# Four heads' last keys in one attention unit, and token groups of 768, 512 and 512 with 512-column products

## The chip, the cores and the metric

The program runs on one core of a Trainium2 chip. The metric is the device time of one execution in microseconds (us). PE is TensorE, which multiplies; PEld is its row of weight loads, shown beside PE; DVE is VectorE, ACT is ScalarE, and SP is the engine whose queue issues every DMA here.

## What is computed

Attention with a sigmoid in place of the softmax (4 batches, 12 heads, 448 tokens, 64 values a head), and behind it two feed-forward layers over all 4 x 448 = 1792 tokens. All arrays are fp32; the layers' weights arrive as 64-bit numbers.

```python
scores = scale * np.matmul(q, k.transpose(0, 1, 3, 2)) - np.log(S)
attn = 1.0 / (1.0 + np.exp(-scores))
x = np.matmul(attn, v)               # then to (1792 tokens, 768)
...
h = x @ w_in                         # 768 -> 2048
g = s * np.maximum(h, 0.0) ** 2 + b
x = g @ w_out                        # 2048 -> 768
...
h = x @ w_in2
g = np.maximum(h, 0.0) + alpha * np.minimum(h, 0.0)
out = g @ w_out2
```

## The kernel before

**Attention.** Two heads make a pair; there are 24 pairs, and each has its K and Q (one tile, 64 rows a head) and its V in a buffer of four. A pair's 448 keys are cut into chunks `c` = 0 to 3 of 128, 128, 128 and 64 keys, and one chunk of one pair is a unit `u`. In a unit the array is used as four quadrants of 64 x 64: `emit_qk` (L234) gives one fp32 product to each quadrant (two heads `j`, two halves `h` of the chunk), `emit_sig` (L248) takes the sigmoid of the scores on ACT, and `emit_av` (L257) gives again four products, two units later. A unit with `c` = 3 has only 64 keys, so it has `h` = 0 alone: two products of scores and two of values. One fp32 product shows as two records in the profile, since it goes over the array twice. `emit_x` (L274) adds the two halves of a finished pair on ACT and DVE. Sixteen units `conv_step` (L307) also turn a weight block from 64 to 32 bits on DVE (`convert`, L123). The loads of pair `q+3` are written in the third unit of pair `q` (L319), so ten units before the first product that reads them.

**Layers.** The tokens go in two groups (`PASSES`, L20) of 896, two batches of 448 each, through each layer `m`. In a pass the 16 blocks of `w_in` are 16 steps and the 6 x 3 cuts of `w_out` are 18 steps (`PER` = 34). Every fp32 operand is split into two numbers of a narrower format (fp32r) whose sum it is, `hi` and `lo`; a chunk of 128 x 128 weights then takes three products for each batch, hi x hi, hi x lo and lo x hi, all into one accumulator: that is `three` (L339), six products of 448 columns. Each product loads its weights anew.

**What feeds the steps.** `split_unit` (L170) makes `hi` on ACT and `lo` on DVE from a 32-bit weight block, two steps ahead; `fetch` (L433) starts the load of a block two steps before that, or converts it where it is used for the first time (`JUST`). `ahead` (L454) converts the first blocks of the second layer in steps 36 to 66. `in_evac` (L360) takes a step's sums out of PSUM, applies the layer's function and splits the result `g`; the `s` and `b` of the first layer are put on after the second product, with a sum that two more columns of `g` (of ones) give (L377, L403). Two PSUM pools of two tiles take turns, so four accumulators are in hand. The order on every engine is the order in which the code is written.

Of the kernel before, what the change touches and what calls it, by code (L numbers as in the profile page):

```python
# [16 lines left out]
P = 128  # L17
OUT_CUTS = [(0, 6), (6, 11), (11, 16)]

PASSES = [(0, 0), (0, 1), (1, 0), (1, 1)]  # L20
# [13 lines left out]
def tile_kernel(  # L34
# [23 lines left out]
    T2 = 2 * S  # L58
    NCUT = len(OUT_CUTS)
    PER = NFC + NK * NCUT  # L60
    LAST = S - (NCH - 1) * P
# [9 lines left out]
    wrawp = pool("wraw", 3)  # L71
    whlp = pool("whl", 3)
    tp = pool("tp", 3)
# [10 lines left out]
    def t_tile(name):  # L84
        return tp.tile([P, T2], F32, tag="t", name=name)

    def g_tile(fc, name="g"):
        return gp.tile([P, 2 * T2 + 2], F32, tag=f"g{fc}", name=f"{name}{fc}")

# [10 lines left out]
    bsum = const.tile([P, NK], F32, name="bsum")  # L100
# [90 lines left out]

    def x_tile(kc):
        x[kc] = xp.tile([P, 2, 2, S], F32R, tag=f"x{kc}", name=f"x{kc}")
        return x[kc]

    def x_store(key, shape_cols, name):
        if key not in x_dram:
            x_dram[key] = dram.tile([P, 2, S], F32, tag=name, name=name)
        return x_dram[key]


    NU = B * NPR * NCH
# [14 lines left out]
    def where(u):  # L217
        q, c = divmod(u, NCH)
        bb, pr = divmod(q, NPR)
        return q, bb, pr, c  # L220
# [13 lines left out]
    def emit_qk(u):  # L234
        q, bb, pr, c = where(u)
        t = kqt[q]
        sc = acc_tile("sc")
        for h in range(2 if c < NCH - 1 else 1):
            for j in range(2):
                rows = slice(j * D, (j + 1) * D)  # L240
                keys = slice(c * P + h * D, c * P + (h + 1) * D)
                nc.tensor.matmul(  # L242
                    sc[h * D : (h + 1) * D, j, :S], t[rows, keys], t[rows, S:],
                    start=True, stop=True,
                )
        sct[u] = sc

    def emit_sig(u):  # L248
        c = u % NCH
        n = P if c < NCH - 1 else LAST  # L250
        sg = buffer("sg", T2).rearrange("p (j s) -> p j s", j=2)
        nc.scalar.activation(  # L252
            sg[:n], sct.pop(u)[:n, :, :S], AF.Sigmoid, bias=bias_t[:n, 0:1], scale=QKSCALE
        )
        sgt[u] = sg

    def emit_av(u):  # L257
        q, bb, pr, c = where(u)
        if c == 0:
            avt[q] = av_tile("av")  # L260
        sg = sgt.pop(u)

        for h in range(2 if c < NCH - 1 else 1):
            for j in range(2):
                keys = slice(h * D, (h + 1) * D)
                nc.tensor.matmul(  # L266
                    avt[q][j * D : (j + 1) * D, h, :S],
                    vtt[q][keys, j, c, :],
                    sg[keys, j, :],
                    start=(c == 0),  # L270
                    stop=(c == NCH - 1 - h),
                )

    def emit_x(q):  # L274
# [5 lines left out]
        if bb < 2:  # L280
            if bb == 0:
                x_tile(pr)
            split(x[pr][:, 1, bb], x[pr][:, 0, bb], t, "V")
        else:
            stores.append((x_store((0, 1, pr), S, f"xa{pr}")[:, bb - 2], t))
# [10 lines left out]
    nc.scalar.activation(bsum[:, 0:1], bias_t, AF.Sigmoid)  # L296
# [10 lines left out]
    conv_step = {4 + (k * 88) // NFC: k for k in range(NFC)}  # L307
    for u in range(NU + 2):
# [8 lines left out]
        if u % NCH == 1 and u > NCH:  # L317
            emit_x(u // NCH - 1)
        if u % NCH == 2:  # L319
            load_kq(u // NCH + 3)  # L320
            load_v(u // NCH + 3)
# [27 lines left out]
    def in_mm(fc, i):  # L349
        hp[fc] = (acc_tile, av_tile)[fc % 2]("hps")  # L350
        w = whl.pop(i)
        for kc in range(NK):
            cols = slice(kc * P, (kc + 1) * P)
            three(
                hp[fc], (S, S), (w[:, 0, cols], w[:, 1, cols]),
                [[x[kc][:, e, bk] for bk in range(2)] for e in range(2)],
                kc == 0, kc == NK - 1,
            )

    def in_evac(m, p, fc):  # L360
        h = hp.pop(fc)[:, :, :S]
        t = t_tile("t")
        t3 = t.rearrange("p (b s) -> p b s", b=2)
        if m == 0:
            nc.scalar.activation(t3, h, AF.Relu)  # L365
            nc.scalar.activation(t, t, AF.Square)  # L366
        else:
            n = t_tile("n")
            nc.scalar.activation(t3, h, AF.Relu)  # L369
            nc.scalar.activation(n.rearrange("p (b s) -> p b s", b=2), h, AF.Relu, scale=-1.0)  # L370
            nc.vector.scalar_tensor_tensor(  # L371
                out=t, in0=n, scalar=nal_t[:, fc : fc + 1], in1=t, op0=ALU.mult, op1=ALU.add
            )
        gt = g_tile(fc)
        if (m, p) == PASSES[0]:

            nc.vector.memset(gt[:, 2 * T2 :], 1.0)  # L377
        gt = gt.bitcast(F32R)
        split(gt[:, T2 : 2 * T2], gt[:, :T2], t, "VA"[m])
        g[fc] = gt  # L380

    def out_mm(dc, cut, i, sums):
        c0, c1 = OUT_CUTS[cut]
        if c0 == 0:
            op_[dc] = (acc_tile, av_tile)[dc % 2]("ops")
        w = whl.pop(i)
        for fc in range(c0, c1):
            o = (fc - c0) * P
            gt = g[fc]
            three(  # L390
                op_[dc], (S, S + 2 if sums else S), (w[:, 0, o : o + P], w[:, 1, o : o + P]),
                [[gt[:, :S], gt[:, S:T2]], [gt[:, T2 : 3 * S], gt[:, 3 * S :]]],
                fc == 0, fc == NFC - 1,
            )

    def out_evac(m, p, dc):
        o = op_.pop(dc)
        t = t_tile("o")
        t3 = t.rearrange("p (b s) -> p b s", b=2)
        if m == 0:  # L400

            if p == 0:
                nc.scalar.activation(  # L403
                    bsum[:, dc : dc + 1], o[:, 1, S : S + 1], AF.Copy, scale=b_t[:, 0:1]
                )
            nc.scalar.activation(
                t3, o[:, :, :S], AF.Identity, scale=s_t[:, 0:1], bias=bsum[:, dc : dc + 1]
            )
            dst = x_store((1, p, dc), T2, f"x2_{p}_{dc}").rearrange("p b s -> p (b s)")
        else:  # L410
            nc.scalar.copy(t3, o[:, :, :S])  # L411
            dst = out[dc * P : (dc + 1) * P, p * T2 : (p + 1) * T2]
        stores.append((dst, t))

    def load_xr(key):
        xr[key] = t_tile("xr")
        nc.sync.dma_start(out=xr[key], in_=x_dram[key].rearrange("p b s -> p (b s)"))

    def make_x(key):
        t = x_tile(key[2])  # L420
        split(
            t[:, 1].rearrange("p b s -> p (b s)"), t[:, 0].rearrange("p b s -> p (b s)"),
            xr.pop(key), "A",
        )
# [29 lines left out]
    ahead = {PER + 2 + 2 * k: PER + k for k in range(NFC)}  # L454

    n_split, n_fetch = 2, 4
    pend = None
    for n, st in enumerate(steps):
# [4 lines left out]
        if kind == "in":  # L463
            in_mm(c, n)
        else:
            out_mm(c, cut, n, o == 0)
# [64 lines left out]
```

## Time and profile before

| | |
|---|---|
| runs of the kernel | 1100.80, 1102.32, 1100.18 us; median 1100.8 |
| the profiled execution's own time | 1100.52 us |
| span of its profile | 1098.7 us |
| attention, from the first product to the first product of the layers | 4.20 to 151.05 us |
| eight phases of the layers (in and out, four passes) | 116.93, 117.11, 119.04, 117.37, 119.03, 117.37, 119.03 and 117.38 us |
| from the last product to the span's end | 4.4 us |
| busy share of the span | PE 99%, PEld 85%, DVE 41%, ACT 39% |

The span is read from left to right as attention, then for each layer and pass a phase `hps` (16 steps, w_in) and a phase `ops` (18 steps, w_out). A matmul's end in the profile is modelled, so its record is longer than the time to the next one; the spacing of starts, or a phase's time over its count, tells what one product costs. The granted clock of TensorE is 1.00, that is 2.4 GHz, in every window asked for.

### The profile page before, as it was taken

How to read it: one execution, taken by the hardware profiler on the slowest of the kernel's cores; microseconds unless marked ns; L12 is line 12 of the kernel's file. 1: busy time of each engine (PE TensorE's matmuls, PEld its weight loads, DVE VectorE, ACT ScalarE, POOL GpSimd, SP SyncE). 2: the span in 40 equal slices, each digit the busy share in tenths (PEclk: the TensorE clock that was granted, in tenths of full speed). 3: DMA queues.
4: the chain of work that ended last, by engine and by line, in shares of the span. 5: the costliest groups of instructions: out<-in, count | busy, mean ns of one | idle time of the engine just before them, and what ended most of it. 6: DMA issues, size and time to landing. Idle time of an engine off the chain costs nothing.

```text
span 1098.7 us, 14184 instructions
## 1 busy us (share of the span) xinstructions
PE 1090.1 (99%) x5952; PEld 930.7 (85%) x5952; DVE 449.6 (41%) x567; ACT 433.9 (39%) x519; POOL 0.2 (0%) x4
## 2 busy tenths in 40 slices
PE   8999999999999999999999999999999999999998
PEld 3444469999999999999999999999999999999997
DVE  3664433346455144544333244375552234431110
ACT  6777753334333134342323244453331344431110
POOL 0000000000000000000000000000000000000000
PEclk9999999999999999999999999999999999999999
DMA  6878720004677433344565511146773111122210
GB/s 248 303 266 309 241 111 1 1 11 145 216 212 223 146 99 120 117 137 141 185 211 187 180 53 48 44 118 184 242 220 116 60 58 58 41 65 67 84 55 34
DMA packets 46864, 147.22 MB, mean 134 GB/s; under 512 B 5584, under 2 KB 7120, under 8 KB 46800
## 3 DMA queue, kind: packets, MB, share of 16 engines
q1 hardware_dynamic: 46800, 146.31, 40.9%
q8 instruction: 47, 0.77, 0.3%
q14 instruction: 17, 0.14, 0.0%
HBM read 107.36 MB, written 38.93 MB: 133 GB/s over the span
## 4 chain that ended last, share of the span: by engine, by line
PE 99%; DMA 0%; ACT 0%; issue 0%
PE hps L344 43%; PE ops L344 43%; PE sc L242 7%; PE av L266 7%; DMA ga<-in_kq 0%; ACT o L411 0%
## 5 line engine op out<-in xcount | busy, mean ns | idle before, releaser
L344 PE MATMUL hps<-x,whl 128*128 128x448 f32 x2304 | 474.6, 367 | 0.0
L344 PE MATMUL ops<-g,whl 128*128 128x448 f32 (+1 forms) x2304 | 469.9, 365 | 0.0
L344 PEld LDWEIGHTS hps<-x,whl 128*128 128x128 f32 x2304 | 432.5, 188 | 42.0 <-issue 0.7
L344 PEld LDWEIGHTS ops<-g,whl 128*128 128x128 f32 x2304 | 432.6, 188 | 36.6
L95 DVE TENSOR_TENSOR whl<-wraw,whl 128x768 fp32r<-128x768 f32 (+1 forms) x120 | 108.3, 902 | 272.4 <-ACT whl L92 272.4
L92 ACT CAST whl<-wraw 128x768 fp32r<-128x768 f32 (+1 forms) x120 | 94.5, 787 | 204.3 <-PE ops L344 186.7
L242 PE MATMUL sc<-ga 64*64 64x448 f32 x672 | 143.9, 555 | 4.2 <-DMA ga<-in_kq 4.2
L266 PE MATMUL av<-ga,ga 64*64 64x448 f32 x672 | 142.2, 540 | 0.0
L252 ACT ACTIVATE ga<-sc,bias_t 128x896 f32<-128x896 f32 x96 | 96.6, 1007 | 40.8 <-PE sc L242 28.9
L365 ACT ACTIVATE t<-hps 128x896 f32<-128x896 f32 x32 | 29.4, 918 | 145.1 <-PE hps L344 145.1
L95 DVE TENSOR_TENSOR g<-t,g 128x896 fp32r<-128x896 f32 x64 | 69.9, 1093 | 33.4 <-ACT g L92 32.3
L242 PEld LDWEIGHTS sc<-ga 64*64 64x64 f32 x672 | 44.6, 134 | 44.5 <-issue 34.8
L371 DVE SCALAR_TENSOR_TENSOR t<-n,nal_t,t 128x896 f32<-128x896 f32 x32 | 36.9, 1152 | 104.1 <-ACT n L370 104.1
L266 PEld LDWEIGHTS av<-ga,ga 64*64 64x64 f32 x672 | 44.9, 133 | 40.1 <-issue 39.3
L94 DVE CAST g<-t 128x896 fp32r<-128x896 f32 x32 | 20.1, 627 | 130.8 <-ACT t L366 130.8
L369 ACT ACTIVATE t<-hps 128x896 f32<-128x896 f32 x32 | 29.4, 918 | 93.1 <-PE hps L344 93.1
L140 DVE SCALAR_TENSOR_TENSOR cva<-r,cva 128x768 f32<-128x768 f32 (+1 forms) x68 | 61.7, 907 | 0.6
L92 ACT CAST g<-t 128x896 fp32r<-128x896 f32 x32 | 30.1, 942 | 39.0 <-DVE t L371 39.0
L134 ACT ACTIVATE cva<-r 128x768 f32<-128x768 f32 (+1 forms) x52 | 44.4, 853 | 0.0
L411 ACT COPY o<-ops 128x896 f32<-128x896 f32 x12 | 10.9, 907 | 70.8 <-PE ops L344 57.1
L279 DVE TENSOR_TENSOR xo<-av,xo 128x448 f32<-128x448 f32 x24 | 15.0, 625 | 57.4 <-ACT xo L278 57.3
L148 DVE SCALAR_TENSOR_TENSOR wraw<-cva,wraw 128x640 uint32<-128x640 uint32 (+1 forms) x36 | 31.3, 870 | 1.2
(26 smaller groups left out, 242.9 us busy)
## 6 DMA issues: line engine op xcount, KB each, us to landing
r<-in_w_in SPq DMA_DIRECT2D x32, 768.0 KB, 5.4
wraw<-w SPq DMA_DIRECT2D x60, 384.0 KB, 3.0
r<-in_w_out SPq DMA_DIRECT2D x24, 640.0 KB, 4.8
ga<-in_kq SPq DMA_DIRECT2D x24, 448.0 KB, 6.6
r<-in_w_out SPq DMA_DIRECT2D x12, 768.0 KB, 5.5
w<-wraw SPq DMA_DIRECT2D x24, 320.0 KB, 5.7
wraw<-w SPq DMA_DIRECT2D x24, 320.0 KB, 3.0
ga<-in_vt SPq DMA_DIRECT2D x24, 256.0 KB, 6.8
```

Source lines behind the costliest of these rows:

```text
L92: nc.scalar.copy(hi, src)
L95: nc.vector.tensor_tensor(out=lo, in0=src, in1=hi.bitcast(F32), op=ALU.subtract)
L134: nc.scalar.activation(a.bitcast(F32), hi.bitcast(F32), AF.Relu, scale=-(2.0**-80))
L140: nc.vector.scalar_tensor_tensor(out=a.bitcast(F32), in0=hi.bitcast(F32), scalar=2.0**-112, in1=a.bitcast(F32), op0=ALU.mult, op1=ALU.max,)
L148: nc.vector.scalar_tensor_tensor(out=u, in0=a, scalar=3, in1=u, op0=ALU.logical_shift_left, op1=ALU.bitwise_or,)
L242: nc.tensor.matmul(sc[h * D : (h + 1) * D, j, :S], t[rows, keys], t[rows, S:], start=True, stop=True,)
L252: nc.scalar.activation(sg[:n], sct.pop(u)[:n, :, :S], AF.Sigmoid, bias=bias_t[:n, 0:1], scale=QKSCALE)
L266: nc.tensor.matmul(avt[q][j * D : (j + 1) * D, h, :S], vtt[q][keys, j, c, :], sg[keys, j, :], start=(c == 0), stop=(c == NCH - 1 - h),)
L344: nc.tensor.matmul(dst[:, bk, :c], w[a], mv[m][bk][:, :c], start=first and k == 0, stop=last and k == 2,)
L365: nc.scalar.activation(t3, h, AF.Relu)
L369: nc.scalar.activation(t3, h, AF.Relu)
L371: nc.vector.scalar_tensor_tensor(out=t, in0=n, scalar=nal_t[:, fc : fc + 1], in1=t, op0=ALU.mult, op1=ALU.add)
```

## The change

- A unit with `c` = 3 now takes the last 64 keys of two pairs, the even pair `q` on one half of the quadrants and pair `q+1` on the other: seven units for two pairs, not eight, 84 in all. The loads of pair `q+3` stay in the third unit of pair `q`, which is now eight units ahead of their first product.
- The tokens go in three groups of 768, 512 and 512 (`TOK`). A chunk of a 512-token group takes three products of 512 columns. A chunk of the 768-token group takes five: the last 256 columns of `hi` and of `lo` lie side by side and go as one product of 512 into two halves of a PSUM bank, which `take` adds up afterwards on DVE; only lo x hi of the last 256 columns goes alone.
- Each weight block is loaded and split six times instead of four. `s` and `b` are applied on DVE in `in_evac`, and the two columns of ones go.
- The pools of raw weights, split weights and temporary tiles have four buffers instead of three, raw blocks are fetched one step earlier, and `ahead` converts every fourth step instead of every second.

```diff
-PASSES = [(0, 0), (0, 1), (1, 0), (1, 1)]
+PASSES = [(0, 0), (0, 1), (0, 2), (1, 0), (1, 1), (1, 2)]
+N5 = 512
...
+    REST = B * S - 3 * N5
+    TG = N5 + REST
+    TOK = [TG, N5, N5]
...
-    wrawp = pool("wraw", 3)
-    whlp = pool("whl", 3)
-    tp = pool("tp", 3)
+    wrawp = pool("wraw", 4)
+    whlp = pool("whl", 4)
+    tp = pool("tp", 4)
...
+    def parts(t):
+        return t[:, N5 : N5 + TG], [(t[:, :N5], 0, N5), (t[:, N5 + TG :], N5, TG)]
...
-    NU = B * NPR * NCH
+    order = []
+    for q in range(0, B * NPR, 2):
+        order += [(q, c) for c in range(NCH)] + [(q + 1, c) for c in range(NCH - 1)]
+    NU = len(order)
...
+    def tiles(u):
+        q, c = order[u]
+        if c == NCH - 1:
+            return [(h, q + h, c * P) for h in range(2)]
+        return [(h, q, c * P + h * D) for h in range(2)]
...
-        for h in range(2 if c < NCH - 1 else 1):
+        for h, q, k0 in tiles(u):
...
-        if u % NCH == 2:
-            load_kq(u // NCH + 3)
-            load_v(u // NCH + 3)
+        if u < NU and order[u][1] == 2:
+            load_kq(order[u][0] + 3)
+            load_v(order[u][0] + 3)
...
-    def three(dst, n, w, mv, first, last):
-        for k, (a, m) in enumerate(((0, 1), (0, 0), (1, 1))):
-            for bk in range(2):
-                c = n[bk] if m == 1 else S
-                nc.tensor.matmul(
-                    dst[:, bk, :c], w[a], mv[m][bk][:, :c],
-                    start=first and k == 0, stop=last and k == 2,
-                )
+    def three(dst, p, w, mv, first, last):
+        hi, lo = w
+        nc.tensor.matmul(dst[:, :N5], hi, mv[:, N5 : 2 * N5], start=first, stop=False)
+        nc.tensor.matmul(dst[:, :N5], hi, mv[:, :N5], start=False, stop=False)
+        if p == 0:
+            nc.tensor.matmul(dst[:, N5 : 2 * N5], hi, mv[:, 2 * N5 :], start=first, stop=False)
+        nc.tensor.matmul(dst[:, :N5], lo, mv[:, N5 : 2 * N5], start=False, stop=last)
+        if p == 0:
+            nc.tensor.matmul(dst[:, N5:TG], lo, mv[:, 2 * N5 : N5 + TG], start=False, stop=last)
...
+    def take(h, p, name):
+        t = t_tile(name)[:, : TOK[p]]
+        nc.scalar.copy(t, h[:, : TOK[p]])
+        if p == 0:
+            nc.vector.tensor_tensor(out=t[:, N5:], in0=h[:, TG:], in1=t[:, N5:], op=ALU.add)
+        return t
...
+            if p == 0:
+                t = take(h, p, "t")
+                nc.vector.scalar_tensor_tensor(
+                    out=t, in0=t, scalar=0.0, in1=t, op0=ALU.max, op1=ALU.mult
+                )
+            else:
+                t = t_tile("t")[:, :N5]
+                nc.scalar.activation(t, h[:, :N5], AF.Relu)
+                nc.scalar.activation(t, t, AF.Square)
+            nc.vector.tensor_scalar(
+                out=t, in0=t, scalar1=s_t[:, 0:1], scalar2=b_t[:, 0:1], op0=ALU.mult, op1=ALU.add
...
-        split(gt[:, T2 : 2 * T2], gt[:, :T2], t, "VA"[m])
+        split_to(g[fc], t, 0, "A" if p == 0 else "V")
...
-    ahead = {PER + 2 + 2 * k: PER + k for k in range(NFC)}
-    n_split, n_fetch = 2, 4
+    ahead = {PER + 2 + 4 * k: PER + k for k in range(NFC)}
+    n_split, n_fetch = 2, 5
```

PE in the attention, second and third pair, before (`sc` scores, `av` values; ga_93 to ga_96 hold K and Q of four pairs, ga_97 to ga_101 sigmoids, ga_102 to ga_105 V):

```order
L266 MATMUL av<-ga_98,ga_102 64x448 x4
L242 MATMUL sc<-ga_94 64x448 x4
L266 MATMUL av<-ga_99,ga_102 64x448 x4
L242 MATMUL sc<-ga_94 64x448 x4
L266 MATMUL av<-ga_100,ga_102 64x448 x2
L242 MATMUL sc<-ga_94 64x448 x4
L266 MATMUL av<-ga_101,ga_103 64x448 x4
L242 MATMUL sc<-ga_94 64x448 x2
L266 MATMUL av<-ga_97,ga_103 64x448 x4
L242 MATMUL sc<-ga_95 64x448 x4
```

The same place of the changed kernel:

```order
L276 MATMUL sc<-ga_93 64x448 x2
L276 MATMUL sc<-ga_94 64x448 x2
L302 MATMUL av<-ga_98,ga_102 64x448 x4
L276 MATMUL sc<-ga_94 64x448 x4
L302 MATMUL av<-ga_99,ga_102 64x448 x4
L276 MATMUL sc<-ga_94 64x448 x4
L302 MATMUL av<-ga_100,ga_102 64x448 x2
L302 MATMUL av<-ga_100,ga_103 64x448 x2
L276 MATMUL sc<-ga_94 64x448 x4
L302 MATMUL av<-ga_101,ga_103 64x448 x4
L276 MATMUL sc<-ga_95 64x448 x4
```

The two products that stood alone (x2) now stand beside two of the next pair, whose buffer is thus first read one unit before its own first chunk.

PE at the beginning of the first layer, before (`hps` the accumulator, x_ the tokens of one chunk of 128 inputs; the last row of the attention stands ahead):

```order
L266 MATMUL av<-ga_97,ga_105 64x448 x2
L344 MATMUL hps<-x_189,whl 128x448 x6
L344 MATMUL hps<-x_234,whl 128x448 x6
L344 MATMUL hps<-x_288,whl 128x448 x6
L344 MATMUL hps<-x_342,whl 128x448 x6
```

The same place of the changed kernel, in its group of 768 tokens:

```order
L302 MATMUL av<-ga_100,ga_105 64x448 x4
L382 MATMUL hps<-x_194,whl 128x512
L383 MATMUL hps<-x_194,whl 128x512
L385 MATMUL hps<-x_194,whl 128x512
L386 MATMUL hps<-x_194,whl 128x512
L388 MATMUL hps<-x_194,whl 128x256
L382 MATMUL hps<-x_232,whl 128x512
```

Six products of 448 became four of 512 and one of 256 here; in the groups of 512 tokens the rows L382, L383 and L386 alone repeat.

DVE in the second pass of the first layer, two steps of which one converts a block ahead, before (`g` the split results, `whl` the split weights, `cw` the converted block):

```order
L94 CAST g_3257<-t 128x896
L95 TENSOR_TENSOR g_3257<-t,g_3257 128x896
L95 TENSOR_TENSOR whl<-wraw,whl 128x768
L94 CAST g_3305<-t 128x896
L95 TENSOR_TENSOR g_3305<-t,g_3305 128x896
L95 TENSOR_TENSOR whl<-wraw,whl 128x768
L140 SCALAR_TENSOR_TENSOR cva<-r_3107,cva 128x768
L145 TENSOR_SCALAR cw<-r_3107 128x768
L148 SCALAR_TENSOR_TENSOR cw<-cva,cw 128x768
```

Two such steps of the changed kernel, in its first group of 512 tokens:

```order
L417 TENSOR_SCALAR t<-t,s_t,b_t 128x512
L210 CAST g_3151<-t 128x512
L215 TENSOR_TENSOR g_3151<-t,g_3151 128x512
L101 TENSOR_TENSOR whl<-wraw,whl 128x768
L146 SCALAR_TENSOR_TENSOR cva<-r_2897,cva 128x768
L151 TENSOR_SCALAR cw<-r_2897 128x768
L154 SCALAR_TENSOR_TENSOR cw<-cva,cw 128x768
L417 TENSOR_SCALAR t<-t,s_t,b_t 128x512
L210 CAST g_3192<-t 128x512
L215 TENSOR_TENSOR g_3192<-t,g_3192 128x512
L101 TENSOR_TENSOR whl<-wraw,whl 128x768
```

A step handles 512 columns of results and not 896, with one operation more, while its weight split is as large as it was; the conversion stands in one step of four.

## Rows read from the trace of the kernel before

**Rows 1.** The page: engines' busy time (share) x instructions; the chain's shares.

```profile
PE 1090.1 (99%) x5952; PEld 930.7 (85%) x5952; DVE 449.6 (41%) x567; ACT 433.9 (39%) x519; POOL 0.2 (0%) x4
PE 99%; DMA 0%; ACT 0%; issue 0%
```

**Rows 2.** The chain in order of time: start, length (us), what.

```profile
0.73 3.42 DMA ga<-in_kq
4.20 4.76 PE sc L242 x24
...
18.00 0.38 PE av L266 x3
...
72.12 0.38 PE av L266 x3
...
151.05 116.93 PE hps L344 x576
267.98 117.11 PE ops L344 x576
385.09 119.04 PE hps L344 x576
504.13 117.37 PE ops L344 x576
...
976.93 117.38 PE ops L344 x576
1094.34 0.91 ACT o L411
```

**Rows 3.** Waits: engine, line waited for: us in total, times, longest; all of PE's.

```profile
PE sc L242 <- DMA ga<-in_kq: 4.2, 1, 4.2
```

**Rows 4.** The page's groups, weight loads: xcount | busy us, mean ns | idle before.

```profile
L344 PEld LDWEIGHTS hps<-x,whl 128*128 128x128 f32 x2304 | 432.5, 188 | 42.0 <-issue 0.7
L344 PEld LDWEIGHTS ops<-g,whl 128*128 128x128 f32 x2304 | 432.6, 188 | 36.6
L242 PEld LDWEIGHTS sc<-ga 64*64 64x64 f32 x672 | 44.6, 134 | 44.5 <-issue 34.8
```

**Rows 5.** Windows: stretch, length, PE, PEld, DVE, ACT, POOL busy, clock, DMA share, GB/s.

```profile
4.00:151.00 147.00, 146.80 (x1345) 65.66 (x1345) 73.76 (x113) 107.61 (x121) 0.00 (x0) 1.00 0.77 270
385.00:504.00 119.00, 119.00 (x578) 108.07 (x577) 55.73 (x67) 46.60 (x55) 0.00 (x0) 1.00 0.38 125
```

**Rows 6.** Windows within the attention, same columns.

```profile
96.00:108.00 12.00, 12.00 (x116) 5.36 (x112) 4.97 (x7) 8.90 (x10) 0.00 (x0) 1.00 1.03 402
```

**Rows 7.** SP's issues from 20 us (pairs 5 and 6): start, us, what.

```profile
24.79 0.33 SPq L120 DMA_DIRECT2D r<-in_w_in  x1
25.78 0.33 SPq L158 DMA_DIRECT2D w<-ga  x1
26.20 0.38 SPq L226 DMA_DIRECT2D ga<-in_kq  x1
...
27.69 0.76 SPq L226 DMA_DIRECT2D ga<-in_kq  x1
```

**Rows 8.** PE's timeline at pair 5's first product, and landing times of attention's loads.

```profile
34.44 0.55 PE L242 MATMUL sc<-ga 64*64 64x448 f32 x3
...
DMA to landing us min/median/max: 2.9/6.6/9.1
```

**Rows 9.** Groups by form, ACT and DVE: xcount | busy us, mean ns | idle before.

```profile
L252 ACT ACTIVATE ga<-sc,bias_t 128x896 f32<-128x896 f32 x72 | 72.6, 1008 | 29.7 <-PE sc L242 17.8 <-PE av L266 10.0 <-ACT xo L278 0.4
L95 DVE TENSOR_TENSOR whl<-wraw,whl 128x768 fp32r<-128x768 f32 x72 | 68.7, 954 | 118.0 <-ACT whl L92 118.0
L92 ACT CAST whl<-wraw 128x768 fp32r<-128x768 f32 x72 | 59.7, 829 | 120.2 <-PE ops L344 109.9 <-issue 10.3
L140 DVE SCALAR_TENSOR_TENSOR cva<-r,cva 128x768 f32<-128x768 f32 x44 | 42.0, 956 | 0.6
L134 ACT ACTIVATE cva<-r 128x768 f32<-128x768 f32 x28 | 25.4, 907 | 0.0
L278 ACT COPY xo<-av 128x448 f32<-128x448 f32 x24 | 12.6, 523 | 0.5 <-PE av L266 0.5
L95 DVE TENSOR_TENSOR x<-xo,x 128x448 fp32r<-128x448 f32 x12 | 7.5, 625 | 0.4
L94 DVE CAST x<-xo 128x448 fp32r<-128x448 f32 x12 | 4.7, 394 | 0.4
L145 DVE TENSOR_SCALAR cw<-r 128x768 uint32<-128x768 uint32 x16 | 8.9, 554 | 0.0
L148 DVE SCALAR_TENSOR_TENSOR cw<-cva,cw 128x768 uint32<-128x768 uint32 x16 | 15.3, 959 | 0.6
```

More of the change, by code (lines that the diff above doesn't have):

```diff
@@ L234, in emit_qk @@
     def emit_qk(u):
[L235 to L236 removed]
         sc = acc_tile("sc")
[L238 removed]
+        for h, q, k0 in tiles(u):
             for j in range(2):
                 rows = slice(j * D, (j + 1) * D)
[L241 removed]
                 nc.tensor.matmul(
[L243 removed]
+                    sc[h * D : (h + 1) * D, j, :S],
+                    kqt[q][rows, k0 : k0 + D],
+                    kqt[q][rows, S:],
                     start=True, stop=True,
@@ L257, in emit_av @@
     def emit_av(u):
-        q, bb, pr, c = where(u)
-        if c == 0:
-            avt[q] = av_tile("av")
+        c = order[u][1]
         sg = sgt.pop(u)
-        for h in range(2 if c < NCH - 1 else 1):
+        for h, q, _ in tiles(u):
+            if q not in avt:
+                avt[q] = av_tile("av")
+            first = c == (NCH - 1 if q % 2 and h else 0)
+            last = c == (NCH - 1 if not q % 2 and not h else NCH - 2)
             for j in range(2):
@@ L269, in emit_av @@
                     sg[keys, j, :],
-                    start=(c == 0),
-                    stop=(c == NCH - 1 - h),
+                    start=first, stop=last,
                 )
@@ L279, in emit_x @@
         nc.vector.tensor_tensor(out=t, in0=av[:, 1, :S], in1=t, op=ALU.add)
[L280 to L285, printed above, removed]
+        if bb == 0:
+            x_tile(pr)
+        for p in range(3):
+            a, e = max(bb * S, TOK0[p]), min((bb + 1) * S, TOK0[p] + TOK[p])
+            if a < e:
+                src = t[:, a - bb * S : e - bb * S]
+                if p == 0:
+                    split_to(x[pr], src, a, "V")
+                else:
+                    stores.append((x_store(0, p, pr)[:, a - TOK0[p] : e - TOK0[p]], src))
     def flush_stores():
@@ L306, in tile_kernel @@
     next64()
-    conv_step = {4 + (k * 88) // NFC: k for k in range(NFC)}
+    conv_step = {4 + (k * (NU - 8)) // NFC: k for k in range(NFC)}
     for u in range(NU + 2):
@@ L316, in tile_kernel @@
         store32()
-        if u % NCH == 1 and u > NCH:
-            emit_x(u // NCH - 1)
-        if u % NCH == 2:
-            load_kq(u // NCH + 3)
-            load_v(u // NCH + 3)
+        if u >= 2:
+            q, c = order[u - 2]
+            if c == NCH - 1 - q % 2:
+                emit_x(q)
+        if u < NU and order[u][1] == 2:
+            load_kq(order[u][0] + 3)
+            load_v(order[u][0] + 3)
         if u in conv_step:
@@ L396, in out_evac @@
     def out_evac(m, p, dc):
-        o = op_.pop(dc)
-        t = t_tile("o")
-        t3 = t.rearrange("p (b s) -> p b s", b=2)
+        t = take(op_.pop(dc), p, "o")
         if m == 0:
[L402 to L409, printed above, removed]
-        else:
-            nc.scalar.copy(t3, o[:, :, :S])
-            dst = out[dc * P : (dc + 1) * P, p * T2 : (p + 1) * T2]
+            dst = x_store(1, p, dc)
+        else:
+            dst = out[dc * P : (dc + 1) * P, TOK0[p] : TOK0[p] + TOK[p]]
@@ L413, in out_evac @@
         stores.append((dst, t))
     def load_xr(key):
-        xr[key] = t_tile("xr")
-        nc.sync.dma_start(out=xr[key], in_=x_dram[key].rearrange("p b s -> p (b s)"))
+        xr[key] = t_tile("xr")[:, : TOK[key[1]]]
+        nc.sync.dma_start(out=xr[key], in_=x_dram[key])
     def make_x(key):
[L420 to L424, printed above, removed]
+        split_to(x_tile(key[2]), xr.pop(key), 0, "A")
```

108 lines of the change are left out of this document (58 added, 50 removed).

## The prediction

> **What bounds the kernel now.** First the engines' busy time: PE is busy 99% of the span, DVE 41%, ACT 39% [rows 1]. Then the chain of waits: all but its ends is PE, and PE waits once in the whole program, 4.2 us for the first K and Q [rows 2, 3]. So only what shortens PE's own row counts, and the question is what one product costs. There are two kinds.
>
> In the attention the chain shows the same point of the rhythm at 18.00 and at 72.12 us [rows 2], nine pairs of heads later: 54.12 / 9 = 6.013 us a pair. A pair has four units, each a round trip of scores and values; in rounds of the four quadrants that is 4 x 4 = 16, of 375.8 ns. A product goes over the array twice, and 2 x 448 columns at 2.4 GHz (the granted clock is 1.00 [rows 5]) are 373.3 ns. Here a product costs its columns and 2.5 ns, and the unit with two quadrants idle costs as much as a full one: with cheaper short units the pair would need 14 rounds, 5.26 us.
>
> In the layers a phase takes 576 products: 116.93 to 119.04 us [rows 2], so 203.0 to 206.7 ns each, 204.7 in the mean of the eight. But 448 columns at 2.4 GHz are 186.7 ns. What fills the other 18? The weight loads: 188 ns each, and the row of loads is idle only 42.0 and 36.6 us over 2304 of them [rows 4], that is 18 and 16 ns. Load and gap together, 432.5 + 42.0 = 474.5 us, are the whole time of the four `hps` phases. I read a chain: a load begins when the product before it has begun, takes 188 ns, and its own product follows 16 to 18 ns behind. In the attention a load of half the columns takes 134 ns [rows 4] under a product of 376, so nothing waits for it. **The layers are thus bound by the weight loads at 448 columns**, just above what the columns need, and a product of 512 (213.3 ns, and 2.5 as in the attention: 215.8) would be bound by its columns, with the load below it.
>
> **Attention, step by step.** 96 units become 84. Twelve units of 4 rounds at 375.8 ns go: 12 x 1.503 = 18.0 us. ACT has to follow: in two pairs seven sigmoids of 1.008 and two copies of 0.523 [rows 9] are 8.1 us under 7 x 1.503 = 10.5 us of PE; it is 77% busy, as before.
> What could come late is a load. It is written eight units ahead of its use, not ten: 12.0 us, not 15.0. In SP's queue it stands behind the reload of a 64-bit block, which waits for the conversion on DVE, and behind the block's store. Where conversion and the end of a pair meet in the unit before, that costs most: the load of pair 5 (counted from 0) is issued at 26.20 and first used at 34.44 [rows 7, 8], 8.2 us later. Take 3.0 from it and 5.2 us remain, against a landing of 6.6 us in the median and 9.1 at most [rows 8]. In the new order units 8 and 61 have that coincidence, each one unit ahead of a load. Each costs between nothing (a landing below 5.2; the shortest is 2.9) and 3.9 us; the median gives 1.4. There is also the denser traffic: the stage moved at a share of 0.77 [rows 5], and the same bytes in 131 us make 0.86; full share does occur, 402 GB/s [rows 6]. I take 2 us for the stage, bounds 0 and 8.
> Attention: 146.85 - 18.0 + 2 = 130.8 us.
>
> **The layers' products.** A chunk of weights had 12 products in its two groups, now 5 + 3 + 3. There are 384 chunks (96 in each of `in` and `out`, in two layers), so 4608 products become 3840 of 512 columns and 384 of 256. The columns are the same in sum, 2,064,384. By the reading above the 512s cost 215.8 ns; the 256s are far below the load and cost what the load chain does, 204.7. No row shows a product of 256 at this size; its bounds are its columns and the gap behind the load, 106.7 + 18 = 125, and 206.7, the dearest phase; I take 204.7, since a load of the same size stands behind it. (125 would save 31 us more, but it needs two loads in 341 ns, and the rows show none of them faster than 188.)
> 3840 x 215.8 = 828.7, and 384 x 204.7 = 78.6: 907.3 us, for 943.3 measured (the eight phases). **Saved: 36.0 us.** By phases: 96 x (4 x 215.8 + 204.7) = 102.5 us for 768 tokens, 96 x 3 x 215.8 = 62.2 for 512. Bounds of the 512: 213.3, the bare columns, and 218, if some of the jitter of 203 to 207 is left: -10 and +8 us.
>
> **What must keep up.** Weight blocks are loaded and split 204 times, not 136. A step of six chunks of 512 tokens is 18 x 215.8 ns = 3.88 us. DVE in it, by the nearest rows scaled to 512 columns [rows 9]: weight split 0.95, the new `s`, `b` operation 0.37 (554 at 768), cast 0.45 (394 at 448), difference 0.71 (625 at 448): 2.5 us, and every fourth step a conversion of 0.956 + 0.554 + 0.959 = 2.5, so 3.1 in the mean. ACT: split 0.83 and two operations of 0.60 (523 at 448), 2.0. Both fit; a step with a conversion takes DVE 5.0, but splits are two steps ahead. A fetch of 384 KB per 3.88 us is 101 GB/s, far below the 402 that was moved.
> In the 768-token group the step is 6.41 us. DVE: addition 0.4, two operations of 0.96 and 0.55, differences 1.1, split 0.95 and a wait for ACT's cast of 0.8, 4.8 in all; in the five steps 11 to 15 of each layer, which convert too, 7.2, so DVE falls 4 us behind under a lead of two steps, 12.8. I take 0.5 us for all of it, bounds 0 and 6. The two columns of ones and the bias chain go from ACT and DVE, which hid them: nothing. The last copy is 512 columns, not 896, 0.60 for 0.91, and its store is smaller: the tail is 4.0 for 4.4.
>
> **The sum** against the profiled execution, whose span is 1098.7 and whose own time 1100.52, 0.3 below the median of the runs: 4.2 + 130.8 + 907.3 + 0.5 + 4.0 = 1046.8, and 1.8 around the span: 1048.6. I say **1049 us**, 52 less.
>
> **The rivals.**
> *A fixed price on every product.* If the 18 ns are not the load but come on top of the columns, whatever they are, the 512s cost 231.4 and the 256s 124.8: 888.6 + 47.9 = 936.5 us, 29.2 more than forecast: 1078. For it: the gap is there in every phase. Against: the attention's products show 2.5 ns.
> *Columns alone.* If fp32r streams more slowly than one column a cycle, 204.7 for 448, equal columns cost equal time, the layers stay at 943.3, and only the attention gains: 1085. Against it speaks the attention's rhythm, which keeps the clock. A page would have it likewise: the Trainium skill, TensorE: Matmul & The Clock Gate, gives a gap of columns / 2.4 + 2.5 ns (section "Back-to-back issue gap") and a load of columns / 1.2, 107 ns here (section "LDWEIGHTS (loading the stationary operand)"), so no load would bind, and 384 products fewer would save 1 us, an estimate from that page. The trace does not agree on either: 188 ns a load, and 203 to 207 ns where its gap gives 189.
> *The loads hold the attention.* If pairs come in as late as the traffic lets them and the shorter lead fails at every pair, the stage stays near its old length, and up to 16 of the 18 us are lost: 1057 to 1065. It decides where lag and landing exceed 12.0 us in most pairs; for pair 5 they make 34.44 - 26.20 too short, for the rest the only wait in rows 3 speaks against it.
> *The feed falls behind: slower.* Place: the 64 `in` steps of the 512-token groups. If ACT and DVE wait for each other in every step, their times add up: 2.0 + 2.5 and a quarter of a conversion (2.5, and 0.9 on ACT) in the first layer, 5.4 us; 4.9 in the second, where an operation of 0.71 stands for the 0.37 and nothing is converted. The mean, 5.1, is 1.2 above the step: +77 us, 1126. From 3.88 us a step it costs, and from 4.73 (54 us over 64 steps on top) the change is slower than before. Against it: in a window with the same code DVE is busy 55.7 and ACT 46.6 of 119 us [rows 5] and PE does not wait.
>
> **How the numbers follow.** Forecast 0.76; fixed price 0.09; columns alone 0.04; attention held 0.07; feed 0.04. The forecast's own range: down 10 for the columns' lower bound, of which I take half since the attention shows 2.5 ns, and 2 for no late load: 1042; up 8 by the attention and 8 by the jitter, not both whole: 1058. With the attention held it reaches 1066. What is left out is the fixed price, columns alone, the feed and a little below, 0.2. So 1042 to 1066. A measurement tells 0.2%, 2.2 us, from no change. Faster than that: all cases but the feed, 0.96. Of the feed's 0.04 I give 0.01 to a loss that just eats the gain, and 0.03 to slower.
>
> **What would show it.** The phases: 102.5 and 62.2 us, without waits on PE. Loads still at 188 ns, but with 28 ns between them under a product of 512, and the product after a 256 starting about 205 ns later. If the fixed price is right, the phases are 100.8 and 66.6. The attention ends at 135 us, with one or two short waits for a K and Q load, near units 9 to 17 and 62 to 70; if it ends at 150 the loads hold it. Waits of PE for `whl` in the 512-token groups would show the feed. The forecast falls if a 512 costs over 218 ns or the attention loses over 8 us to loads.

## The result, and the profile after

The changed kernel took 1061.1 us in the median of four runs (1060.42 to 1061.98), the one before 1100.5 beside it: a ratio of 0.964, 95% interval 0.9623 to 0.9657. That is 39.4 us less; forecast were 52, in a range that holds the time near its upper end. The profiled execution took 1060.63 us with a span of 1058.8. Its parts, by the trace:

| part of the span | before | forecast | after |
|---|---|---|---|
| to the first product | 4.2 | 4.2 | 4.1 |
| attention | 146.8 | 130.8 | 128.6 |
| layers, with the feed | 943.3 | 907.8 | 922.6 |
| tail | 4.4 | 4.0 | 3.7 |

So the attention came out 2.2 us better than forecast and the layers 14.8 us worse. The page, in the order of [rows 1]:

```profile
PE 1051.1 (99%) x5568; PEld 814.4 (77%) x5568; DVE 594.4 (56%) x879; ACT 448.9 (42%) x625; POOL 0.2 (0%) x4
```

PE is as full as it was; DVE has 145 us more to do, and PE waits for none of it. All that PE waits for is still one load, as in [rows 3]:

```profile
PE sc L276 <- DMA ga<-in_kq: 4.0, 1, 4.0
```

The windows (columns as in [rows 5]) of the attention, of a phase with 768 tokens and of two with 512:

```profile
4.00:132.60 128.60, 128.55 (x1344) 48.64 (x1344) 72.64 (x119) 95.71 (x109) 0.00 (x0) 1.00 0.88 311
132.70:232.70 100.00, 100.00 (x484) 83.36 (x481) 67.67 (x102) 38.12 (x50) 0.00 (x0) 1.00 0.13 38
332.80:398.00 65.20, 65.20 (x289) 53.99 (x289) 47.42 (x74) 34.04 (x51) 0.00 (x0) 1.00 0.46 150
398.10:463.30 65.20, 65.20 (x289) 53.99 (x288) 30.67 (x40) 23.25 (x35) 0.00 (x0) 1.00 0.71 239
```

A phase of 768 tokens takes 100.0 us (forecast 102.5), one of 512 takes 65.3 (forecast 62.2), and each kind is alike within 0.13. The two phases of 512 tokens take the same time although DVE is busy 47.4 us of one and 30.7 of the other and the DMA share is 0.46 and 0.71, so the price of a product does not follow what the other engines or the transfers do. The products are neither what I said of the 512s nor of the 256s. PE's and PEld's timeline, start and length, around one product of 256 (L388) in a 768-token phase:

```profile
200.09 0.39 PE L386 MATMUL hps<-x,whl 128*128 128x512 f32 x1
200.10 0.19 PEld L388 LDWEIGHTS hps<-x,whl 128*128 128x128 f32 x1
...
200.32 0.28 PE L388 MATMUL hps<-x,whl 128*128 128x256 f32 x1
200.32 0.19 PEld L382 LDWEIGHTS hps<-x,whl 128*128 128x128 f32 x1
200.44 0.40 PE L382 MATMUL hps<-x,whl 128*128 128x512 f32 x1
200.44 0.19 PEld L383 LDWEIGHTS hps<-x,whl 128*128 128x128 f32 x1
```

The load for L382 begins at 200.32 and is drawn to 200.51, but its product begins at 200.44. A product does not wait for the end of its load's record. With that the chain that I read out of [rows 4] is gone: the 256 costs 117 ns, not 204.7. And in a 512-token phase, where the load (188 ns) has 25 ns to spare, the products still do not come at 215.8:

```profile
350.21 0.39 PE L386 MATMUL hps<-x,whl 128*128 128x512 f32 x1
350.44 0.39 PE L382 MATMUL hps<-x,whl 128*128 128x512 f32 x1
350.67 0.39 PE L383 MATMUL hps<-x,whl 128*128 128x512 f32 x1
350.89 0.39 PE L386 MATMUL hps<-x,whl 128*128 128x512 f32 x1
```

Three spacings in 0.68 us; over a phase, 65.28 us / 288 = 226.7 ns, 13.3 over the columns (512 at 2.4 GHz, 213.3). The runs below ask what these 13.3 ns are, whether the two parts of the change add up, and whether the feed and the loads were as near the edge as I had priced them.

### The profile page after: what moved, and what is told of

Its sections match the earlier page's. It is cut to its first block, busy times and chain, and to the rows that moved or that the text cites. A ratio compares the mean times of both kernels' runs of the same rounds, so it can differ in the third digit from the quotient of the medians.

```text
span 1058.8 us, 14149 instructions
## 1 busy us (share of the span) xinstructions
PE 1051.1 (99%) x5568; PEld 814.4 (77%) x5568; DVE 594.4 (56%) x879; ACT 448.9 (42%) x625; POOL 0.2 (0%) x4
## 4 chain that ended last, share of the span: by engine, by line
PE 99%; DMA 0%; ACT 0%; issue 0%
PE hps L383 12%; PE ops L383 12%; PE hps L382 12%; PE ops L382 12%; PE ops L386 12%; PE hps L386 12%; PE sc L276 6%; PE av L302 6%; PE ops L385 4%; PE hps L385 4%; PE ops L388 2%; PE hps L388 2%; DMA ga<-in_kq 0%; ACT o L400 0%
## 5 line engine op out<-in xcount | busy, mean ns | idle before, releaser
L101 DVE TENSOR_TENSOR whl<-wraw,whl 128x768 fp32r<-128x768 f32 (+1 forms) x188 | 167.7, 902 | 133.7 <-ACT whl L98 132.9
L383 PE MATMUL hps<-x,whl 128*128 128x512 f32 x576 | 225.0, 391 | 0.0
L383 PE MATMUL ops<-g,whl 128*128 128x512 f32 x576 | 224.9, 391 | 0.0
L382 PE MATMUL hps<-x,whl 128*128 128x512 f32 x576 | 224.9, 390 | 0.0
L382 PE MATMUL ops<-g,whl 128*128 128x512 f32 x576 | 224.8, 390 | 0.0
L386 PE MATMUL hps<-x,whl 128*128 128x512 f32 x576 | 224.7, 390 | 0.0
L386 PE MATMUL ops<-g,whl 128*128 128x512 f32 x576 | 224.7, 390 | 0.0
L98 ACT CAST whl<-wraw 128x768 fp32r<-128x768 f32 (+1 forms) x188 | 146.8, 792 | 40.5 <-PE ops L386 26.1
L382 PEld LDWEIGHTS hps<-x,whl 128*128 128x128 f32 x576 | 108.1, 188 | 24.0 <-issue 0.7
L386 PEld LDWEIGHTS ops<-g,whl 128*128 128x128 f32 x576 | 108.1, 188 | 23.4
L386 PEld LDWEIGHTS hps<-x,whl 128*128 128x128 f32 x576 | 108.1, 188 | 23.4
L382 PEld LDWEIGHTS ops<-g,whl 128*128 128x128 f32 x576 | 108.1, 188 | 23.2
L383 PEld LDWEIGHTS ops<-g,whl 128*128 128x128 f32 x576 | 108.3, 188 | 14.9
L383 PEld LDWEIGHTS hps<-x,whl 128*128 128x128 f32 x576 | 108.3, 188 | 14.8
L400 ACT COPY o<-ops 128x512 f32<-128x512 f32 (+1 forms) x36 | 23.7, 659 | 169.4 <-PE ops L386 104.8
L215 DVE TENSOR_TENSOR g<-t,g 128x512 fp32r<-128x512 f32 (+1 forms) x128 | 77.2, 624 | 31.9 <-ACT g L208 29.7
L276 PE MATMUL sc<-ga 64*64 64x448 f32 x672 | 79.3, 550 | 4.0 <-DMA ga<-in_kq 4.0
L302 PE MATMUL av<-ga,ga 64*64 64x448 f32 x672 | 77.1, 536 | 0.0
L385 PE MATMUL ops<-g,whl 128*128 128x512 f32 x192 | 75.7, 394 | 0.0
L385 PE MATMUL hps<-x,whl 128*128 128x512 f32 x192 | 75.6, 394 | 0.0
```

Source lines behind the costliest of these rows:

```text
L98: nc.scalar.copy(hi, src)
L101: nc.vector.tensor_tensor(out=lo, in0=src, in1=hi.bitcast(F32), op=ALU.subtract)
L215: nc.vector.tensor_tensor(out=lo[:, a - o : e - o], in0=src[:, a - c0 : e - c0], in1=hi[:, a - c0 : e - c0].bitcast(F32), op=ALU.subtract,)
L276: nc.tensor.matmul(sc[h * D : (h + 1) * D, j, :S], kqt[q][rows, k0 : k0 + D], kqt[q][rows, S:], start=True, stop=True,)
L302: nc.tensor.matmul(avt[q][j * D : (j + 1) * D, h, :S], vtt[q][keys, j, c, :], sg[keys, j, :], start=first, stop=last,)
L382: nc.tensor.matmul(dst[:, :N5], hi, mv[:, N5 : 2 * N5], start=first, stop=False)
```

## The two parts alone

**Attention alone.** The kernel before with `order`, `tiles`, `emit_qk`, `emit_sig`, `emit_av`, the loads and `conv_step` of the changed one.

> The kernel before with the attention part of the change alone: the last 64 keys of two pairs in one unit, 84 units; tokens stay in two groups of 896. Theory: the twelve units that go are worth their rounds whatever the layers do, 12 x 4 x 375.8 ns = 18.0 us, and the loads come in time, as the changed kernel's stage of 128.6 us (146.85 before) lets one think: 1082.3, bounds 1081 and 1083.5. Rival: the layers' code after the attention or its buffers gave part of the 18 us (the changed kernel has four temporary tiles for three): then over 1084.

Measured: 1084.8 us in the median (1082.65 to 1085.98), ratio 0.9849, interval 0.9829 to 0.9869, that is 1082.0 to 1086.4. The profiled execution, 1082.65, has a stage of 129.0 us and the eight phases of [rows 2] unchanged within 0.1, so it is what the theory says. The median is not: it lies above the theory's bounds, where the rival was expected. The other executions are up to 3.3 us longer, without a profile. The same stage took 128.6 to 130.4 us in the profiled executions of this document, so it can hold 1.8 of them; the rest stays open.

**Token groups alone.** The changed kernel with the 96 units of before.

> The changed kernel with the attention of before (96 units), so the token groups of 768, 512 and 512 alone. Theory: the two parts add, 1061.1 + 18.2 = 1079.3, with the layers' phases as in the changed kernel, 100.0 and 65.3 us. Rival: the parts help or hinder each other (weights and buffers at the passage into the layers): a sum off by over 2 us.

Measured: 1078.8 us (1078.20 to 1079.85), ratio 0.9797, interval 0.9777 to 0.9817; the phases are those of the changed kernel (100.0 and 65.3 us), the stage 146.9. By the profiled executions 1079.25 - 1060.63 = 18.6 us go to the attention, and 1082.65 - 1060.63 = 22.0 to the token groups, 40.6 for the 39.9 of both together. By the medians they are 17.7 and 23.7, 41.4 for 39.4. **The parts add, within 0.7 to 2 us.**

## What a product costs

**Sizes.** One execution of the changed kernel with `SIZE[now[0]]` columns in most products of the 512-token groups, one size a phase; the rest of the columns is left out:

```diff
...
+        if p > 0:
+            n = N5 if first or last else SIZE[now[0]]
+            nc.tensor.matmul(dst[:, :n], hi, mv[:, N5 : N5 + n], start=first, stop=False)
+            nc.tensor.matmul(dst[:, :n], hi, mv[:, :n], start=False, stop=False)
+            nc.tensor.matmul(dst[:, :n], lo, mv[:, N5 : N5 + n], start=False, stop=last)
+            return
...
```

> The changed kernel, where in the 512-token groups only the first and the last chunk of each accumulation take 512 columns, and the products between take, phase by phase, 448, 384, 320, 256, 480, 192, 128 and 64 columns; the rest of the columns is left out. The spacing of equal products in a row is read. Theory of the prediction (a load begins with the product before it and must end before its own): nothing under 204 ns, at any size. Theory of a fixed price, from the 226.7 ns of a 512 (13.3 over its columns): 213 at 480, 200 at 448, 173 at 384, 147 at 320, 120 at 256, and at 192, 128 and 64 a floor set by the loads near the 114 to 117 ns that follow a 256 in the changed kernel. If the price goes with the columns: 212, 198, 170, 142, 113 instead.

PE's timeline in the phases of 448, 256, 480 and 128 columns (L388, L389 and L390 are the three products of a chunk):

```profile
353.87 0.36 PE L390 MATMUL hps<-x,whl 128*128 128x448 f32 x1
354.07 0.36 PE L388 MATMUL hps<-x,whl 128*128 128x448 f32 x1
354.27 0.36 PE L389 MATMUL hps<-x,whl 128*128 128x448 f32 x1
...
515.11 0.28 PE L390 MATMUL ops<-g,whl 128*128 128x256 f32 x1
515.23 0.28 PE L388 MATMUL ops<-g,whl 128*128 128x256 f32 x1
515.35 0.28 PE L389 MATMUL ops<-g,whl 128*128 128x256 f32 x1
515.47 0.28 PE L390 MATMUL ops<-g,whl 128*128 128x256 f32 x1
...
801.47 0.38 PE L388 MATMUL hps<-x,whl 128*128 128x480 f32 x1
801.69 0.37 PE L389 MATMUL hps<-x,whl 128*128 128x480 f32 x1
801.90 0.38 PE L390 MATMUL hps<-x,whl 128*128 128x480 f32 x1
...
879.07 0.28 PE L389 MATMUL hps<-x,whl 128*128 128x128 f32 x1
879.18 0.28 PE L390 MATMUL hps<-x,whl 128*128 128x128 f32 x1
879.29 0.27 PE L388 MATMUL hps<-x,whl 128*128 128x128 f32 x1
```

| columns | median spacing, ns | columns / 2.4 GHz | over |
|---|---|---|---|
| 480 | 216 | 200.0 | 16 |
| 448 | 203 | 186.7 | 16 |
| 384 | 173 | 160.0 | 13 |
| 320 | 146.5 | 133.3 | 13 |
| 256 | 120 | 106.7 | 13 |
| 192 | 111 | 80.0 | floor |
| 128 | 111 | 53.3 | floor |
| 64 | 112 while the clock was full | 26.7 | floor |

The prediction's reading is refuted: nothing is held at 204. A product costs its columns and 13 to 16 ns, down to a floor near 111 that the size no longer moves; at 480 and 448 it is 3 ns more than the fixed price of 13.3 gives. I take the floor for the load, though no run changed the load at these sizes. A load's record is 188 ns for 128 columns and 134 for 64 [rows 4], which is 0.84 ns a column, 108 for 128, and some 80 ns that do not hold up the next one. The Trainium skill, TensorE: Matmul & The Clock Gate, section "LDWEIGHTS (loading the stationary operand)", gives columns / 1.2, an estimate of 107 ns for 128 columns; the floor of 111 agrees, and I had set the record's 188 against it.

**Shapes.** One execution with eight ways to do the same 512 columns, one a phase, for instance (parts of the sums are left out or replaced):

```diff
...
+            mm = nc.tensor.matmul
+            a, b = mv[:, N5 : 2 * N5], mv[:, :N5]
+            d, e = dst[:, :N5], dst[:, N5 : 2 * N5]
+            if now[0] == ("in", 0, 1):
+                for u, v in ((hi, a), (hi, b), (lo, a)):
+                    mm(d[:64], u[:, :64], v, start=False, stop=False)
+                return
...
+            if now[0] == ("in", 0, 2):
+                mm(d, hi, a, start=False, stop=False)
+                mm(e, hi, b, start=True, stop=True)
+                mm(d, lo, a, start=False, stop=False)
+                return
...
```

> The changed kernel, where in the 512-token groups the products between the first and the last chunk are changed phase by phase, all of 512 columns: weights of 64 columns (first layer, group 2, in), weights of 64 rows (out), the second of three products into another bank (group 3, in), three times the same product (out), weights of 32 columns (second layer, group 2, in), all products started anew in another bank and not accumulated (out), no change (group 3, in), plain fp32 in place of fp32r (out). Sums are wrong or left out for these. The spacing is read against 226.7 ns. If the 13.3 ns over the columns come from loading the weights into the array, they shrink with the weights' columns: 6.7 at 64 and 3.3 at 32, and rows change nothing. If they come from accumulating, the products started anew show 215.8. If from the bank, the product in another bank differs. If from fp32r itself, plain fp32 shows 2 x 213.3 and 2.5 ns, 429, a record, as the attention does; if from the full array, 440.

Median spacing: 229.5 ns with weights of 64 columns and 233 with 32 (full ones beside them in those phases 227 and 234), 227 with 64 rows, 226.7 in the mean with one product of three in another bank, with three equal products, with products started anew, and without a change. Plain fp32 has 429 a record, 2 x 213.3 and 2.3; it has two records a product, so a product goes over its columns four times; by the rounds of 375.8 ns it does so in the attention too, where the kernel's description says twice. The chain (start, length, what) with weights of 64 columns, equal products, weights of 32 columns, products started anew, and fp32:

```profile
335.02 2.76 PE hps L389 x12
...
534.31 9.52 PE ops L402 x42
...
803.73 2.78 PE hps L406 x12
...
866.51 9.53 PE ops L410 x42
...
997.08 36.05 PE ops L414 x84
```

The loads of the narrow weights are shorter, here those of 32 columns (groups of one phase: xcount | busy us, mean ns | idle before), and nothing comes of it:

```profile
L406 PEld LDWEIGHTS hps<-x,whl 128*32 128x32 f32 x177 | 19.2, 108 | 20.9
```

So the price does not fall with a shorter load or less of the array, and it is not the bank, the accumulation or the change of operands. The next thing to vary is the type.

**The type.** The changed kernel with bf16 in place of fp32r for all `hi` and `lo` parts:

```diff
-F32R = mybir.dt.float32r
+F32R = mybir.dt.bfloat16
...
-        nc.vector.tensor_tensor(out=lo, in0=src, in1=hi.bitcast(F32), op=ALU.subtract)
+        nc.vector.tensor_tensor(out=lo, in0=src, in1=hi, op=ALU.subtract)
...
```

> The changed kernel with all hi and lo parts of weights, tokens and results in bf16 instead of fp32r, nothing else; less precise, since two bf16 parts keep fewer bits. Theory: the 13.3 ns that a product of 512 takes over its columns belong to fp32r, since plain fp32 shows 2.3 (429 a record of two times 213.3): 215.8 ns a 512, 62.2 us a phase of a 512-token group, and the program about 45 us shorter, 1016. Rival: they belong to a full array with new weights in every product, whatever the type, and plain fp32 only hides them behind its two passes: 226.7 ns again, 1061.

Measured: 1010.9 us (1010.09 to 1012.12), ratio 0.9177, interval 0.9161 to 0.9192. A phase of 512 tokens takes 62.16 us, 215.8 ns a product: the number of the forecast, with another type. One of 768 takes 93.4, so a chunk is 972.5 ns and its 256 costs 972.5 - 4 x 215.8 = 109. The time is 5 us below the 1016 expected, which had counted 13.3 ns a product: in fp32r the products of the 768-token phases cost 16.4 in the mean over their columns, and lose that too. The windows of such phases:

```profile
134.30:227.60 93.30, 93.30 (x482) 46.93 (x481) 65.63 (x99) 37.93 (x50) 0.00 (x0) 1.00 0.12 37
321.50:383.50 62.00, 62.00 (x289) 28.10 (x288) 47.02 (x73) 33.92 (x51) 0.00 (x0) 1.00 0.49 156
```

The 13.3 ns go with fp32r. With the type, the width of the operands and the load's record (98 ns for 188) changed too; which part of fp32r's handling costs the time is not shown, though the short loads above say that it is not their length. The Trainium skill's gap of columns / 2.4 + 2.5 ns (the page and section named in the prediction), which the page calls the gap of a single product, fits bf16 and fp32 here, and misses fp32r by 8 to 18 ns where no floor binds.

**The kernel before in bf16.** If that is right, the token groups are worth nothing where the price is 2.5 ns:

> The kernel before with all hi and lo parts in bf16 instead of fp32r, nothing else. Theory: what the token groups brought is the price that fp32r puts on every product, so that at a price of 2.5 ns they are worth almost nothing: 4608 products of 448 take 189.2 ns each, 871.8 us for 943.3, that is 1029 us, and the distance to the changed kernel in bf16 (1010.9) is the attention's 18 us alone, where in fp32r it was 39. Rival: a part of the gain is the number of products or the shape itself (fewer passages from product to product, full banks): then the 448s stay above 195 ns and the time is over 1055.

Measured: 1029.35 us (1028.62 to 1029.81), ratio 0.9347, interval 0.9330 to 0.9364. A phase of 576 products takes 108.96 us, 189.2 ns each, and the first two 0.1 to 0.2 more:

```profile
151.50:260.30 108.80, 108.80 (x576) 56.29 (x577) 49.24 (x75) 43.12 (x52) 0.00 (x0) 1.00 0.10 32
```

The layers take 871.9 us here, and 872.2 in the changed kernel in bf16, 1.5 of them in two phases where splits came late: the token groups bring nothing as measured in bf16 and 1.2 us without the late splits, for 20.7 in fp32r. Of the 18.5 us between the two kernels' medians the attention's stage is 16.9 in the profiled executions (146.9 and 130.0). **What the layers' part of the change saves goes with the price per product that fp32r sets; without that price it is about 1 us.**

## Where the price varies

Over a 768-token chunk the five products take 1042 ns, 82 over their columns, where five times 13.3 are 67. And 448 columns cost 203 to 207 ns in the kernel before, 203 in the run over sizes. Two runs were to find the cause.

**Bank by bank.** The order of a chunk's five products changed so that the first bank's three come first:

> The changed kernel where the five products of a chunk in the 768-token group go bank by bank (three into the first, then two into the second) in place of the order hi, hi, hi, lo, lo. In the changed kernel such a phase takes 100.0 us, 1042 ns a chunk, 82 over its columns where five times 13.3 are 67. Theory: the bank does not matter, as a product in another bank showed 226.7: 100.0 us and 1061 again, within 1.5. Rival: it is the passage from bank to bank: 98.6 us and 1055.

Measured: 1061.95 us (1060.34 to 1062.73), ratio 0.9641, interval 0.9627 to 0.9655, phases of 100.0 and 65.3 as before. The order of the banks is not it.

**Starts.** One execution, products of 448 columns read or written from shifted columns; the rest of the columns is left out:

> The changed kernel where in the 512-token groups the products between the first and the last chunk take 448 columns (the rest is left out), with the first column read shifted phase by phase: 0; 64; 0 and 64 in turn; 32; 16; 8; then the first column written shifted by 64, without and with the same shift of the columns read. A 448 took 203.0 to 206.7 ns in the kernel before and 202 in the run over sizes, where the fixed price gives 200. Theory: where a product starts to read or write sets the 2 to 7 ns on top, so that the phases differ, 200 to 207, and the one with two starts in turn looks like before. Rival: they come from 448 itself: all phases alike near 202.

Medians: 206 ns without a shift, 207 at 64, 206 with 0 and 64 in turn, 204 at 32, 201 at 16, 206 at 8; with the written column shifted 202 and 203. They do differ, by 6 ns. But the phase without a shift is the same code as that of 448 in the run over sizes, and took 206 here and 203 there, one execution each. So neither theory holds: the start alone does not set it. What adds 0 to 7 ns to the 13.3, in a mix of sizes, at 448 or at 480, **stays open**. In bf16 nothing of the kind is seen: 215.8 and 189.2 in every phase, but for the late splits.

## The feed and the loads

**Three buffers.** The changed kernel with pools of three and blocks fetched four steps ahead:

> The changed kernel with three buffers for raw weights, split weights and temporary tiles again, and blocks fetched four steps ahead instead of five. Theory: the feed has room (DVE 2.5 to 3.1 us of a step of 4.08) and the deeper buffers are not what holds it: 1061, within 2, no wait of PE in the layers. Rival: without them PE waits for split weights in the 512-token groups or where the first conversions fall, over 1064.

Measured: 1061.4 us, ratio 0.9638, interval 0.9621 to 0.9655: no different from the changed kernel. The deeper buffers do nothing for the time here. Only the time tells it; PE's waits were not read.

**Conversions moved.** In the changed kernel the loads of pairs 5 and 20, which the prediction had named for units 8 and 61, land 0.24 and 0.27 us before their use, the least of all after the first. SP's issues in the changed kernel, pair 5 at 24.40, behind the reload and the store as in [rows 7]:

```profile
22.98 0.33 SPq L126 DMA_DIRECT2D r<-in_w_in  x1
23.98 0.33 SPq L164 DMA_DIRECT2D w<-ga  x1
24.40 0.38 SPq L263 DMA_DIRECT2D ga<-in_kq  x1
```

It landed at 30.08 and was used at 30.32. In the bf16 run it came 0.8 us late. There the two conversions were moved:

```diff
+    conv_step[6], conv_step[60] = conv_step.pop(8), conv_step.pop(61)
```

> The changed kernel in bf16 with the conversions of units 8 and 61 moved to 6 and 60, so that none meets the end of a pair right ahead of a load. Theory: these two meetings are what made pairs 5 and 20 the tightest (in the changed kernel their K and Q land 0.24 and 0.27 us before use, and in the bf16 run pair 5 comes 0.8 late): both then land at least 1.5 us before use, the attention's wait goes, and the time is 0.8 shorter than 1010.9 at best, which timing can hardly tell. Rival: it is the traffic that makes them late, and they stay as tight.

Pair 5 is now issued at 20.39, not 25.19, and lands 1.9 us before use; pair 20 lands 2.7 before. The stage is 128.8 us, not 130.0:

```profile
18.98 0.33 SPq L126 DMA_DIRECT2D r<-in_w_in  x1
19.97 0.33 SPq L164 DMA_DIRECT2D w<-ga  x1
20.39 0.38 SPq L263 DMA_DIRECT2D ga<-in_kq  x1
```

The meeting of a conversion with the end of a pair was the cause of the late loads, not the traffic. Of the 1.2 us of the stage they are 0.8. The rest is its beginning, which goes at about half the rate of what follows: a row of eight records takes 0.75 us later on, and the first 32 took 5.96 us in the bf16 run and 5.54 with the conversions moved (the windows read a granted clock of 1.00 there all the same):

```profile
4.28 4.76 PE sc L276 x24
9.04 1.20 PE av L302 x8
...
4.40 4.76 PE sc L276 x24
9.15 0.78 PE av L302 x8
```

The time is 1009.9 us (1009.21 to 1010.51), ratio 0.9172, interval 0.9155 to 0.9189; beside 1010.9 that is within what timing tells. It beats both kernels of this case by 4.8 and 8.3%, at the cost of precision, which no run here measured.

## Point by point

- **Attention: right.** Twelve units at 4 rounds of 375.8 ns were 18.0 us; the stage lost 18.2. The 2 us for late loads did not come in the profiled execution, but the two pairs were the right ones, with a quarter of a microsecond to spare; in five other profiled runs of the same stage the products of pair 5 came 0.6 to 1.0 us late. The stage took 129.6 to 130.4 us there, in part by its slow beginning. From issue to use pair 5 had 5.9 us, where I had left it 5.2.
- **The bound of the layers: wrong.** The step that failed is "the layers are thus bound by the weight loads at 448 columns". It rested on one coincidence, 188 ns of load and 16 to 18 of gap that fill a product's time. The load's record includes a part that the next product need not wait for, and what it does hold up, 111 ns at 128 columns by the floor, was far from binding. The rows could have said so: "a load begins when the product before it has begun" is true at any size and shows no wait. And one place in the trace of before speaks against the chain. At the first products of the layers, behind an idle row, the second load begins 0.11 us after the first, whose record is 0.19:

```profile
150.98 0.19 PEld L344 LDWEIGHTS hps<-x,whl 128*128 128x128 f32 x1 [0.70 <-issue]
151.09 0.19 PEld L344 LDWEIGHTS hps<-x,whl 128*128 128x128 f32 x1
```

So a load can follow the one before it after 0.11 us, and two do fit into the 341 ns that the prediction called too short for them.
- **The size of a 512: wrong.** Forecast 215.8, measured 226.7 in the 512-token groups and 231 in the 768-token one (1042 less 117, by four). The 2.5 ns were taken over from fp32 products, a type that does not pay fp32r's price: 2304 x 10.9 + 1536 x 15.4 ns = +48.8 us.
- **The size of a 256: wrong the other way.** Forecast 204.7, measured 117: 384 x 87.7 = -33.7 us. The lower bound of 125 that I had set aside was the nearer one. The two errors leave +15: that the range held the time is luck, since they happen to cancel for the most part; the layers' gain, 20.7 us for 36.0, was a little over half of the forecast.
- **The fixed price, at 0.09, was the nearest mechanism**, at the wrong size: it took the 18 ns of before as the same for all. Its phases, 100.8 and 66.6 us, are nearer to the 100.0 and 65.3 measured than the forecast's; its time, 1078, is 17 us too long, where the forecast's is 12 too short. With 14.8 ns for a product in the mean after (922.6 less 860.2 for the columns, over 4224), of the 20.7 us saved 384 x 18.0 = 6.9 come from fewer products and the other 13.8 from the smaller price of each, 3.3 ns. Why the price is smaller, and so two thirds of what the layers gained, is the part that stays open.
- **Columns alone** would have left the layers at 943: refuted by 922 in fp32r, and nearly true in bf16.
- **The feed: right that it holds.** DVE is busy 47.4 of 65.2 us in the 512-token phase with conversions shown above, and PE waits for none of it.

## What to carry to other kernels

A record's length is not what it holds up: before a load or a matmul is called the bound, look for a place where its successor starts before it ends, or vary the size of one operand and see whether the time follows. Where products of two types run in one kernel, take the price per product from the same type; one run with the sizes changed phase by phase gives the whole curve. Before re-tiling to save a price per product, ask whether another type does not pay it.

## What the runs showed of the hardware

- fp32r of 128 x 128 weights costs 13.3 ns a product over its columns, and 10 to 20 in some arrangements; bf16 and plain fp32 (per record, over twice the columns) cost 2.3 to 2.5. The price does not shrink with the weights' rows or columns, and does not go with the bank, the accumulation or equal operands.
- The price was seen at the full clock alone. In the run over sizes, in a stretch at half clock, fp32r products of 512 came at 427 ns, which is 512 columns at 1.2 GHz and nothing over (the window's clock is the third number from its end):

```profile
921.00:924.50 3.50, 3.50 (x12) 2.92 (x12) 0.20 (x1) 1.44 (x3) 0.00 (x0) 0.50 0.26 88
...
922.39 0.63 PE L390 MATMUL ops<-g,whl 128*128 128x512 f32 x1
922.82 0.63 PE L388 MATMUL ops<-g,whl 128*128 128x512 f32 x1
923.25 0.63 PE L389 MATMUL ops<-g,whl 128*128 128x512 f32 x1
```

- With fp32r the median product comes 111 to 112 ns after the one before it, from 192 columns to 64. In bf16 a 256 took 109, its columns and 2.5 ns, and a load's record is 98 ns.
- In the run over sizes products of 64 columns came at 112 ns each, PE busy throughout by the records; in the window from 920 to 935 us the granted clock was 0.51 (1.2 GHz), and they came at 213 ns: the floor doubles with half the clock.
